# One pool of eight PSUM banks, and both query tiles of a group in one stretch, in a fused sketch-attention and mixture-of-experts attention kernel

## The chip, the cores and the metric

The kernel runs on one core of one Trainium2 chip. The metric is the device time of one execution in microseconds (us). Engines go by their names in the profile: PE (TensorE matmuls), PEld (TensorE weight loads), DVE (VectorE), ACT (ScalarE), POOL (GpSimd), SP (SyncE, which issues the DMAs).

## The reference

Two attention layers follow each other, in float32, for 4 batches of 1088 positions.

```python
# 1. polysketch attention: q, k, v (4, 4 heads, 1088, 32), S1, S2 (8, 32)
phi(x) = outer(S1 @ x, S2 @ x)            # 64 features per position
kv = sum_s phi(k) v^T;  z = sum_s phi(k)
x = (phi(q) @ kv) / (phi(q) @ z + 1e-6)   # heads side by side: (4, 1088, 128)

# 2. four attention experts of head size 64, the two best of them for each position
w = softmax over the two largest of x @ w_gate (sum + 1e-9)
for e in range(4):
    s = causal(x wq[e] @ (x wk[e])^T / 8)
    a = exp(s - max(s));  a /= sum(a) + 1e-9
    out += w_e * (a @ (x wv[e]) @ wo[e])  # w_e is 0 where e was not chosen
```

All four experts are computed for all positions, and the gate multiplies. The output is (4, 1088, 128).

## The kernel before

**Tiles.** The 1088 queries of a batch are nine tiles `i` of 128 (the last, tile 8, has 64). Tile `i` sees `n = 128 * i + 128` keys. The four experts are two groups `g` of two; the two experts `e` of a group lie in the two halves of the partitions of `qk`. Tiles 0 to 7 go in pairs `p` (tiles `2p` and `2p + 1`). For a pair and a group the kernel does the following.

- `scores`: PE multiplies queries by keys in pieces of up to 512 keys into a PSUM tile `sc` (L412). `soften` makes DVE add the causal mask, negate and keep the running minimum `mx` in one pass that also copies the tile to `a` in SBUF (L395), and ACT take the exponential with the sum `z` (L398).
- `turns_of`: PE transposes `a` by blocks of 128 into PSUM tiles `tp` (L477); `evacuate` copies each to `aT`, every third on DVE (L70), the others on ACT (L72).
- `values`: PE multiplies `aT` by the values `vt` into `av[:, 0:256]` (L552).
- `gates`: DVE makes `r = 1 / (z + 1e-9)` (L497, L498), POOL multiplies it by the gate weights into `rb` (two buffers, L501), PE transposes `rb` into `av[:, 256:]` (L507) and ACT copies that to `rs` (L509). DVE multiplies `av` by `rs` into `yT` (L557).
- `output`: PE multiplies `yT` of both groups by `wo` into `po` (L619), a copy to `ob`, and SP issues the write (L624).

Tile 8 has steps of its own: `scores_last` (L449, minimum L464, exponential L466) with both groups in one tile of 128 partitions, and `last_unit`. Pair 0 has `scores_first` (L429).

**PSUM.** The pool `ps_sc` has two tiles of two banks, for scores alone. The pool `ps_tp` has four tiles of one bank, for `tp`, `av`, `po` and everything that the first layer and the projections put there. Tiles of a pool take turns: a new tile waits until the users of the tile that had its place are done.

**Order.** PE's order is written out by hand (`manual_schedule`); a scheduler orders the other engines by the dependences. `prepare(b)` makes the next batch's first layer and projections into pieces with costs (`fill`): `kps`, `qps` (L251, sketches), `kv`, `tq`, `num`, `tx`, `qk` and `vg` (L338). `spend` puts pieces between the transposes, in proportion to the costs in `STEPS`. `units(b)` gives a batch's steps in order, by kind:

- "Q": pair 0, both groups. "P": pair 1, one group. "G": pair 2 or 3, one group. "L": tile 8.
- In the last batch pairs come in the order 1, 3, 2, 0, and "A" and "B" are the two tiles of a "G" as steps of their own.

In a "G" step PE does the scores of the first tile, then `values` of the step before, the scores of the second tile, the outputs of the step before and the transposes of the first tile with pieces between them, then the transposes of the second tile. "Q", "P", "L", "A" and "B" leave their transposes, or half of them, to the next step (`turns`, `turning`).

Of the kernel before, what the change touches and what calls it, by code (L numbers as in the profile page):

```python
# [19 lines left out]
def kernel(  # L20
# [20 lines left out]
    nc = tc.nc  # L41
# [14 lines left out]
    ps_sc = ctx.enter_context(tc.tile_pool(name="ps_sc", bufs=2, space=bass.MemoryType.PSUM))  # L56
    ps_tp = ctx.enter_context(tc.tile_pool(name="ps_tp", bufs=4, space=bass.MemoryType.PSUM))
# [9 lines left out]
    def evacuate(out_, in_):  # L67
        turn[0] += 1
        if turn[0] % 3 == 0:
            nc.vector.tensor_copy(out_, in_)  # L70
        else:
            nc.scalar.copy(out_, in_)  # L72

# [132 lines left out]
    def prepare(b):  # L206
# [7 lines left out]

        def bank(name):
            return ps_tp.tile([128, 512], F32, tag="tp", name=name)
# [176 lines left out]
    def soften(a, src, msk, mx, z, most=3e38):  # L393

        nc.vector.tensor_tensor_reduce(out=a, in0=src, in1=msk, scale=-1.0, scalar=most,  # L395
                                       op0=ALU.add, op1=ALU.min, accum_out=mx)
        if z is not None:
            nc.scalar.activation(out=a, in_=a, func=ACTF.Exp, bias=mx, scale=-1.0, accum_out=z)  # L398

    def scores(b, i, g, qk, z):  # L400

        n = 128 * i + 128
        if n <= 512:
            t = ps_sc.tile([128, 2, 512], F32, tag="sc", name=f"sc{b}_{i}_{g}")
            sc = [t[:, e, :] for e in range(2)]
        else:
            sc = [ps_sc.tile([128, 1024], F32, tag="sc", name=f"sc{b}_{i}_{g}_{e}") for e in range(2)]
        for c0 in range(0, n, 512):
            c1 = min(c0 + 512, n)
            for e in range(2):  # L410
                rows = slice(64 * e, 64 * e + 64)
                nc.tensor.matmul(sc[e][:, c0:c1], qk[rows, g, 128 * i : 128 * i + 128], qk[rows, NG + g, c0:c1],  # L412
                                 start=True, stop=True)
        mx = p4.tile([128, 2], F32, tag="mx", name=f"mx{b}_{i}_{g}")
        width, tag, bufs = (512, "as", 8) if n <= 512 else (S, "a", 4)
        ats = [p4.tile([128, width], F32, tag=tag, name=f"a{b}_{i}_{g}_{e}", bufs=bufs) for e in range(2)]
        for e in range(2):
            soften(ats[e][:, 0:n], sc[e][:, 0:n], mask[:, 1024 - n :], mx[:, e : e + 1], z[:, e : e + 1])
        return ats

    def scores_first(b, qk, zs):

        made = [[[], []] for _ in range(NG)]
        for g in range(NG):
            t = ps_sc.tile([128, 2, 512], F32, tag="sc", name=f"sc{b}_0_{g}")
            for i in range(2):
                for e in range(2):
                    rows = slice(64 * e, 64 * e + 64)
                    nc.tensor.matmul(t[:, e, 128 * i : 256 * i + 128], qk[rows, g, 128 * i : 128 * i + 128],  # L429
                                     qk[rows, NG + g, 0 : 128 * i + 128], start=True, stop=True)  # L430
            mx = p4.tile([128, 2, 2], F32, tag="mx0", name=f"mx{b}_0_{g}")
            a = [p4.tile([128, 512], F32, tag="as", name=f"a{b}_0_{g}_{e}", bufs=8) for e in range(2)]
            for i in range(2):
                for e in range(2):
                    n, dst = 128 * i + 128, a[e][:, 128 * i : 256 * i + 128]
                    soften(dst, t[:, e, 128 * i : 256 * i + 128], mask[:, 1024 - n :], mx[:, i, e : e + 1],
                           zs[g][:, i, e : e + 1])
                    made[g][i].append(dst)
        return made

    def scores_last(b, qk, z):

        sc = [ps_sc.tile([128, 1024], F32, tag="sc", name=f"sc{b}_8_{e}") for e in range(2)]
        ext = [ps_tp.tile([128, 512], F32, tag="tp", name=f"ext{b}_{e}")[:, 0:64] for e in range(2)]

        def some(dst, e, c0, c1):
            rows = slice(64 * e, 64 * e + 64)
            for g in range(NG):
                nc.tensor.matmul(dst[64 * g : 64 * g + 64], qk[rows, g, 1024:], qk[rows, NG + g, c0:c1],  # L449
                                 start=True, stop=True)  # L450

        for e in range(2):
            some(ext[e], e, 1024, S)
        for c in range(0, 1024, 512):
            for e in range(2):
                some(sc[e][:, c : c + 512], e, c, c + 512)
        mx = p4.tile([128, 4], F32, tag="mx8", name=f"mx{b}_8")
        ats = [p4.tile([128, S], F32, tag="a", name=f"a{b}_8_{e}") for e in range(2)]
        for e in range(2):
            soften(ats[e][:, 1024:], ext[e], mask_last, mx[:, 2 + e : 3 + e], None)  # L460
        for e in range(2):

            most = mx[:, e : e + 1]
            nc.vector.tensor_tensor_reduce(out=ats[e][:, 0:1024], in0=sc[e], in1=mask[:, 0:1].to_broadcast([128, 1024]), scale=-1.0,  # L464
                                           scalar=mx[:, 2 + e : 3 + e], op0=ALU.add, op1=ALU.min, accum_out=most)
            nc.scalar.activation(out=ats[e], in_=ats[e], func=ACTF.Exp, bias=most, scale=-1.0, accum_out=z[:, e : e + 1])  # L466
        return ats

    def turns_of(name, i, ats, aT, q0):

        def some(e0, e1, j0, j1):
            tp = ps_tp.tile([128, 512], F32, tag="tp", name=f"tp{name}_{e0}_{j0}")
# [54 lines left out]
    STEPS = (4.2, 2.0, 2.4, 2.4, 2.2, 3.2, 3.2, 4.1)  # L527

    def units(b, qk, vt, gw, gw8):

# [4 lines left out]
        for p in range((NJ - 1) // 2) if b < B - 1 else (1, 3, 2, 0):  # L535
            yT = p2.tile([128, NG, 256], F32, tag="yT", name=f"yT{b}_{p}")
            nk = 2 * (2 * p + 2)
            four = []
            for g in range(NG):
                if p or not g:  # L540
                    aT_all = p2.tile([128, 16 * 256], F32, tag="aT", name=f"aT{b}_{p}_{g}")
                aT = aT_all[:, 0 if p else g * nk * 256 :][:, 0 : nk * 256].rearrange("p (e j s) -> p e j s", e=2, s=256)
# [3 lines left out]
                def values(p=p, g=g, aT=aT, yT=yT, name=name):  # L546
                    av = ps_tp.tile([128, 512], F32, tag="tp", name=f"av{name}")
# [17 lines left out]
                def make(x, p=p, g=g, z=z):  # L565
                    return scores(b, 2 * p + x, g, qk, z[:, x])

                def turns(made, x, p=p, aT=aT, name=name):
                    return turns_of(f"{name}_{x}", 2 * p + x, made[x], aT, 128 * x)

                if p == 0:
                    four.append((z, turns, close))
                elif p == 1:
                    yield "P", make, turns, [close]
                elif b < B - 1:
                    yield "G", make, turns, [close]
                else:
                    yield "A", make, turns, []
                    yield "B", make, turns, [close]
            if four:  # L580
                yield ("Q", lambda x: scores_first(b, qk, [z for z, _, _ in four]),
                       lambda made, x: [f for g in range(NG) for i in range(2) for f in four[g][1](made[0][g], i)],
                       [close for _, _, close in four])
# [3 lines left out]
    def last_unit(b, qk, vt, gw8):  # L587
# [5 lines left out]
        def values():  # L593
            av = ps_tp.tile([128, 512], F32, tag="tp", name=f"av{b}_8")
# [16 lines left out]
        return ("L", lambda x: scores_last(b, qk, z[:, 0]), lambda made, x: turns_of(f"{b}_8", NJ - 1, made[0], aT, 0),  # L611
                [lambda: (gates(f"{b}_8", z, gw8[:, None, :], 128), values)])

    def output(b, p, yT):
        nq, n = (128, 2) if p < NJ // 2 else (64, 1)
        po = ps_tp.tile([128, 512], F32, tag="tp", name=f"po{b}_{p}")
# [10 lines left out]
    with tc.manual_schedule(engines={mybir.EngineType.PE}):  # L627

        warm = ps_tp.tile([128, 512], F32, tag="tp", name="warm")
# [14 lines left out]
        for b in range(B):  # L644
# [13 lines left out]
            else:  # L658
                fill.extend(own)
                lead = sum(c for c, _ in fill) / 2  # L660
            for n, (kind, make, turned, close) in enumerate(units(b, *now)):
                jobs, turns = turns + done, []
                if kind == "L" or kind == "Q" and b == B - 1:
                    for f in jobs:
                        f()
                    jobs = []
                    groups += turning
                    turning = []
                made = {x: make(x) for x in ((0, 1) if kind == "P" else (1,) if kind == "B" else (0,))}
                ends = do_values()  # L670
                spend(0.0, columns=True)
                if kind == "G":
                    made[1] = make(1)
                    jobs += turned(made, 0)
                done = [f for finish, to_gate in ends for f in finish(to_gate)]
                if b + 1 < B:
                    us = share * STEPS[n] + (lead if n == 0 else 0.0)
                else:
                    us = (lead, 1e9, 0.0)[min(n, 2)]
# [13 lines left out]
                for f in turns[:cut]:  # L693
                    f()
# [41 lines left out]
```

## Time and profile before

| what | us |
|---|---|
| median of 3 runs | 398.3 (398.27 to 398.81) |
| the profiled execution | 398.61 |
| its span, first to last instruction | 396.8 |
| PE busy in it | 373.2 (94%) |
| DVE busy | 234.6 (59%) |
| ACT busy | 226.5 (57%) |
| granted TensorE clock, mean | 1.000 |

The span is a little shorter than the execution around it. A row such as `L398 ACT ACTIVATE a<-a,mx 128x256 ... x128 | 98.1, 767 | 59.6 <-DVE mx` reads: line and engine, the operation, what it writes from what, the shape, how many; total busy time in us and the mean of one in ns; then the engine's idle time right before these and what ended most of it. In the list of waits the three numbers are the sum, the number and the longest. In the timeline a row has its start, its length, and in brackets the idle time ahead of it and what ended it. In the chain of waits a row has start, length and the work.

### The profile page before, as it was taken

The numbers are of one execution on the slowest core, as the hardware profiler recorded it, in microseconds if no ns is written. First come the engines' busy times: TensorE is split into PE (matmuls) and PEld (weight loads), VectorE is DVE, ScalarE is ACT, GpSimd is POOL, SyncE is SP. The second block draws the span as 40 slices with busy tenths as digits, with TensorE's granted clock in tenths as the row PEclk, the third lists the DMA queues.
The fourth block names the chain that finished last, engine by engine and source line by source line (L and its number), as shares of the span: only waits on it lengthen the run. The fifth ranks groups of instructions, "written<-read, shape, count | busy, mean of one in ns | idle before, by whom it ended". The sixth has DMA issues, their size and how long they took to land.

```text
span 396.8 us, 8017 instructions
## 1 busy us (share of the span) xinstructions
PE 373.2 (94%) x3152; PEld 265.4 (67%) x3152; DVE 234.6 (59%) x661; ACT 226.5 (57%) x550; POOL 58.7 (15%) x87
## 2 busy tenths in 40 slices
PE   8898999999999999999999999999999999999995
PEld 7764687667665776767664767766756475666673
DVE  6867866555548675366456564555655844745551
ACT  2236666555666656456475656754665565656582
POOL 3400461000001740000000541000000010000010
PEclk9999999999999999999999999999999999999999
DMA  7705022000000000000000000000000000000000
GB/s 192 200 2 170 16 98 71 2 1 15 13 2 0 15 2 5 15 0 15 1 15 0 2 13 7 13 2 0 15 13 2 1 16 6 0 15 2 15 4 26
DMA packets 11349, 9.95 MB, mean 25 GB/s; under 512 B 3632, under 2 KB 10288, under 8 KB 11312
## 3 DMA queue, kind: packets, MB, share of 16 engines
q1 hardware_dynamic: 11296, 9.44, 8.6%
q8 instruction: 24, 0.39, 0.4%
q14 instruction: 13, 0.11, 0.1%
q10 hardware_dynamic: 16, 0.00, 0.0%
HBM read 7.22 MB, written 2.23 MB: 24 GB/s over the span
## 4 chain that ended last, share of the span: by engine, by line
PE 72%; DVE 15%; ACT 9%; issue 2%; DMA 2%; SPq 0%; ACTq 0%; DVEq 0%
PE av L552 16%; PE sc L412 15%; PE tp L477 14%; DVE a L395 7%; ACT a L398 7%; PE qk L326 5%; PE vg L338 3%; PE num L300 3%; PE po L619 3%; PE av L600 3%; PE sc L449 2%; DMA qin<-in_q_dram 2%; DVE qT L223 1%; PE sc L429 1%; PE qps L251 1%
## 5 line engine op out<-in xcount | busy, mean ns | idle before, releaser
L398 ACT ACTIVATE a<-a,mx 128x256 f32<-128x256 f32 (+7 forms) x128 | 98.1, 767 | 59.6 <-DVE mx L395 59.2
L395 DVE CUSTOM_DVE_ANT_0 a<-sc,mask 128x256 f32<-128x256 f32 (+7 forms) x128 | 90.2, 754 | 64.1 <-PE sc L412 62.1
L477 PE MATMUL tp<-ident,a 128*128 128x128 f32 (+1 forms) x648 | 90.1, 276 | 10.6 <-DVE yT L557 6.8
L477 PEld LDWEIGHTS tp<-ident,a 128*128 128x128 f32 (+1 forms) x648 | 72.8, 142 | 26.0 <-DVE yT L557 10.2
L72 ACT COPY aT<-tp 128x512 f32<-128x512 f32 (+3 forms) x119 | 61.6, 544 | 17.9 <-PE tp L477 17.2
L552 PE MATMUL av<-aT,vt 128*64 128x256 f32 (+1 forms) x640 | 67.9, 362 | 0.0
L412 PE MATMUL sc<-qkT 64*128 64x512 f32 (+3 forms) x320 | 67.7, 541 | 0.0
L501 POOL TENSOR_TENSOR rb<-gw,r 128x256 f32<-128x256 f32 (+1 forms) x36 | 21.1, 589 | 297.2 <-DVE r L498 227.2
L552 PEld LDWEIGHTS av<-aT,vt 128*64 128x64 f32 x640 | 43.2, 137 | 31.0 <-issue 10.0
L70 DVE COPY aT<-tp 128x512 f32<-128x512 f32 (+3 forms) x61 | 38.6, 633 | 21.4 <-PE tp L477 21.3
L412 PEld LDWEIGHTS sc<-qkT 64*128 64x128 f32 x320 | 27.9, 186 | 23.7 <-issue 19.9
L326 PE MATMUL qk<-xT,wqk 128*128 128x512 f32 x64 | 31.1, 602 | 0.0
L509 ACT COPY rs<-av 128x256 f32<-128x256 f32 (+1 forms) x36 | 12.1, 356 | 27.7 <-PE av L507 27.6
L398 ACT ACTIVATION_READ_ACCUMULATOR a<-a,mx 128x1 f32 x128 | 23.9, 187 | 0.0
L619 PE MATMUL po<-wo,yT 128*128 128x128 f32 (+1 forms) x144 | 20.4, 281 | 1.7 <-DVE yT L557 1.5
L338 PE MATMUL vg<-wvg,xT 128*128 128x260 f32 (+1 forms) x72 | 20.2, 392 | 1.5 <-DVE vt L70 1.5
L497 DVE TENSOR_SCALAR r<-z 128x4 f32<-128x4 f32 (+1 forms) x36 | 6.3, 176 | 23.5 <-ACT a L398 16.6
L72 ACT COPY qkT<-qk 128x512 f32<-128x512 f32 x20 | 11.7, 585 | 14.4 <-PE qk L326 14.1
L619 PEld LDWEIGHTS po<-wo,yT 128*128 128x128 f32 (+1 forms) x144 | 17.3, 185 | 3.5 <-DVE yT L557 1.9
L300 PE MATMUL num<-kvz,qpT 128*128 128x66 f32 x144 | 17.9, 273 | 0.2 <-ACT qpT L72 0.2
L300 PEld LDWEIGHTS num<-kvz,qpT 128*128 128x128 f32 x144 | 17.1, 192 | 0.9 <-ACT qpT L72 0.5
L326 PEld LDWEIGHTS qk<-xT,wqk 128*128 128x128 f32 x64 | 10.7, 190 | 8.4 <-issue 4.7
(118 smaller groups left out, 392.0 us busy)
## 6 DMA issues: line engine op xcount, KB each, us to landing
kin<-in_k_dram SPq DMA_DIRECT2D x4, 544.0 KB, 4.0
qin<-in_q_dram SPq DMA_DIRECT2D x4, 544.0 KB, 5.1
vin<-in_v_dram SPq DMA_DIRECT2D x16, 128.0 KB, 5.7
out_dram<-ob SPq DMA_DIRECT2D x16, 128.0 KB, 1.8
vtl<-in_v_dram SPq DMA_DIRECT2D x8, 16.0 KB, 3.4
wqk<-in_moe_wq_dram SPq DMA_DIRECT2D x1, 128.0 KB, 5.3
wqk<-in_moe_wk_dram SPq DMA_DIRECT2D x1, 128.0 KB, 3.2
wvg<-in_moe_wv_dram SPq DMA_DIRECT2D x1, 128.0 KB, 3.1
```

The costliest lines, as they stand in the source:

```text
L70: nc.vector.tensor_copy(out_, in_)
L72: nc.scalar.copy(out_, in_)
L300: nc.tensor.matmul(num[:, 66 * (y - 2 * x0) : 66 * (y - 2 * x0) + 66], qpT[:, y], kvz[:, y % 2].rearrange("p h d -> p (h d)"), start=True, ...
L326: nc.tensor.matmul(t, wt(a), xT[:, 512 * c : 512 * c + 512], start=True, stop=True)
L338: nc.tensor.matmul(t[0:m, 0 : E * HD + E], xT[:, 128 * j : 128 * j + m], wvg, start=True, stop=True)
L395: nc.vector.tensor_tensor_reduce(out=a, in0=src, in1=msk, scale=-1.0, scalar=most, op0=ALU.add, op1=ALU.min, accum_out=mx)
L398: nc.scalar.activation(out=a, in_=a, func=ACTF.Exp, bias=mx, scale=-1.0, accum_out=z)
L412: nc.tensor.matmul(sc[e][:, c0:c1], qk[rows, g, 128 * i : 128 * i + 128], qk[rows, NG + g, c0:c1], start=True, stop=True)
L477: nc.tensor.transpose(tp[0:nk, x : x + 128], ats[e][:, 128 * j : 128 * j + nk], ident)
L501: nc.gpsimd.tensor_tensor(out=rb[:, 0 : w // 128].rearrange("p x (e d) -> p x e d", d=HD), in0=gws[:, :, :, None].to_broadcast(wide), in1= ...
L552: nc.tensor.matmul(av[HD * e : HD * e + HD, lo:256], vt[:, j, c : c + HD], aT[:, e, j, lo:256], start=(j == 0), stop=(j == 2 * p + 1))
L619: nc.tensor.matmul(po[0:nq, DM * x : DM * x + DM], yT[:, g, 128 * x : 128 * x + nq], wo_sb[:, g], start=(g == 0), stop=(g == NG - 1))
```

## The change

There is one pool `ps` of eight one-bank tiles, taken in turn in the order of allocation, for everything that lies in PSUM. The scores of a tile are cut into chunks of 512 keys, each with a bank of its own and a pass of its own on DVE, `take`; its minimum starts from that of the chunk before (`mx[:, e, 0:1]`). `soften` is then the exponential alone, after the last chunk. Tile 8's scores are three such chunks.

A step makes the scores of both tiles of its pair in one stretch, before `values`. Pair 1 is one step with both groups, as pair 0 was, so a batch has seven steps. The steps of pairs 0 and 1 are now of kind "G" too: every step but "L" does its own transposes, half of them between the pieces and half after. "L" still leaves its own to the next step. The last batch has the same steps as the others, in its own order of pairs.

```diff
-    ps_sc = ctx.enter_context(tc.tile_pool(name="ps_sc", bufs=2, space=bass.MemoryType.PSUM))
-    ps_tp = ctx.enter_context(tc.tile_pool(name="ps_tp", bufs=4, space=bass.MemoryType.PSUM))
+    ps = ctx.enter_context(tc.tile_pool(name="ps", bufs=8, space=bass.MemoryType.PSUM))
...
+    def bank(name):
+        return ps.tile([128, 512], F32, tag="bank", name=name)
...
-    def soften(a, src, msk, mx, z, most=3e38):
-        nc.vector.tensor_tensor_reduce(out=a, in0=src, in1=msk, scale=-1.0, scalar=most,
+    def take(dst, src, msk, mx, most=3e38):
+        nc.vector.tensor_tensor_reduce(out=dst, in0=src, in1=msk, scale=-1.0, scalar=most,
                                        op0=ALU.add, op1=ALU.min, accum_out=mx)
-        if z is not None:
-            nc.scalar.activation(out=a, in_=a, func=ACTF.Exp, bias=mx, scale=-1.0, accum_out=z)
+
+    def soften(a, mx, z):
+        nc.scalar.activation(out=a, in_=a, func=ACTF.Exp, bias=mx, scale=-1.0, accum_out=z)
 
     def scores(b, i, g, qk, z):
         n = 128 * i + 128
-        if n <= 512:
-            t = ps_sc.tile([128, 2, 512], F32, tag="sc", name=f"sc{b}_{i}_{g}")
-            sc = [t[:, e, :] for e in range(2)]
-        else:
-            sc = [ps_sc.tile([128, 1024], F32, tag="sc", name=f"sc{b}_{i}_{g}_{e}") for e in range(2)]
-        for c0 in range(0, n, 512):
-            c1 = min(c0 + 512, n)
+        mx = p4.tile([128, 2, 2], F32, tag="mx", name=f"mx{b}_{i}_{g}")
+        width, tag, bufs = (512, "as", 8) if n <= 512 else (S, "a", 4)
+        ats = [p4.tile([128, width], F32, tag=tag, name=f"a{b}_{i}_{g}_{e}", bufs=bufs) for e in range(2)]
+        for c in range(0, n, 512):
+            keys = slice(c, min(c + 512, n))
+            sc = [bank(f"sc{b}_{i}_{g}_{c}_{e}")[:, 0 : keys.stop - c] for e in range(2)]
             for e in range(2):
                 rows = slice(64 * e, 64 * e + 64)
-                nc.tensor.matmul(sc[e][:, c0:c1], qk[rows, g, 128 * i : 128 * i + 128], qk[rows, NG + g, c0:c1],
+                nc.tensor.matmul(sc[e], qk[rows, g, 128 * i : 128 * i + 128], qk[rows, NG + g, keys],
                                  start=True, stop=True)
...
-        for e in range(2):
-            soften(ats[e][:, 0:n], sc[e][:, 0:n], mask[:, 1024 - n :], mx[:, e : e + 1], z[:, e : e + 1])
+            for e in range(2):
+                m = mx[:, e, c // 512 : c // 512 + 1]
+                take(ats[e][:, keys], sc[e], mask[:, 1024 - n + c : 1024 - n + keys.stop], m,
+                     mx[:, e, 0:1] if c else 3e38)
+                if keys.stop == n:
+                    soften(ats[e][:, 0:n], m, z[:, e : e + 1])
...
-    STEPS = (4.2, 2.0, 2.4, 2.4, 2.2, 3.2, 3.2, 4.1)
+    STEPS = (4.2, 4.4, 2.4, 2.2, 3.2, 3.2, 4.1)
...
-                if p == 0:
-                    four.append((z, turns, close))
-                elif p == 1:
-                    yield "P", make, turns, [close]
-                elif b < B - 1:
-                    yield "G", make, turns, [close]
-                else:
-                    yield "A", make, turns, []
-                    yield "B", make, turns, [close]
...
+                def make(p=p, g=g, z=z):
+                    if p == 0:
+                        return scores_first(b, g, qk, z)
+                    return [scores(b, 2 * p + x, g, qk, z[:, x]) for x in range(2)]
...
+                makes.append(make)
+                turned.append(turns)
+                closes.append(close)
+                if p > 1 or g == NG - 1:
+                    yield "G", makes, turned, closes
+                    makes, turned, closes = [], [], []
...
-                made = {x: make(x) for x in ((0, 1) if kind == "P" else (1,) if kind == "B" else (0,))}
+            for n, (kind, makes, turned, closes) in enumerate(units(b, *now)):
+                made = [make() for make in makes]
                 ends = do_values()
                 spend(0.0, columns=True)
-                if kind == "G":
-                    made[1] = make(1)
-                    jobs += turned(made, 0)
+                jobs = turns + done
                 done = [f for finish, to_gate in ends for f in finish(to_gate)]
...
+                groups += turning
+                turns, turning = [f for t, m in zip(turned, made) for f in t(m)], []
+                late = turns[len(turns) // 2 :] if kind == "G" else []
+                if kind == "G":
+                    jobs += turns[: len(turns) // 2]
+                    turns = []
```

Chunk by chunk the parts of `scores_first` (now once per group) and `scores_last` change in the same way; `close`, `values` and `output` are as before but for the pool.

## The prediction

> **What bounds the kernel now.** I read first the page's busy line and the shares of the chain that ended last, then PE's waits, then all waits, then instruction forms by width, then the timeline of one step. PE is busy for 94% of the span, at a granted clock of 1.000, and the output DMAs and SP's queue do not appear in the chain: time is PE's instructions plus PE's holes.
>
> ```profile
> PE 373.2 (94%) x3152; PEld 265.4 (67%) x3152; DVE 234.6 (59%) x661; ACT 226.5 (57%) x550; POOL 58.7 (15%) x87
> ...
> PE 72%; DVE 15%; ACT 9%; issue 2%; DMA 2%; SPq 0%; ACTq 0%; DVEq 0%
> ```
> ```profile
> PE tp L477 <- DVE yT L557: 6.8, 11, 0.8
> PE kps L251 <- ACT aT L72: 1.6, 3, 0.8
> PE po L619 <- DVE yT L557: 1.5, 2, 0.8
> PE vg L338 <- DVE vt L70: 1.5, 2, 0.7
> ```
> The largest wait of PE is that of a transpose tile `tp` for `yT`, which it does not read: it needs the PSUM bank. The timeline of tile 7's step shows it.
> ```profile
> 103.58 0.37 ACT L509 COPY rs<-av 128x256 f32<-128x256 f32 x1 [2.33 <-PE av L507]
> ...
> 104.54 1.15 ACT L398 ACTIVATE a<-a,mx 128x1024 f32<-128x1024 f32 x1 [0.58 <-DVE mx L395]
> 105.50 0.08 DVE L395 DVE_READ_ACCUMULATOR2_ANT mx<- 128x1 f32 x1
> 105.50 0.42 DVE L557 TENSOR_TENSOR yT<-av,rs 128x256 f32<-128x256 f32 x1
> ...
> 105.98 0.66 PE L477 MATMUL tp<-ident,a 128*128 128x128 f32 x4 [0.77 <-DVE yT L557]
> ```
> `rs` was ready at 103.95, but `yT` stood on DVE behind two minimum passes of 1.22 us and ran at 105.50; the bank of `av`, four allocations back, came free only then. Adding the spaces between PE's records over the whole timeline gives 20.2 us: 4.3 before 22 us (the first loads), 8.4 in the twelve "G" steps of batches 0 to 2 (3.2, 2.65, 2.6), 3.8 in their "Q" and "P" steps, 3.75 in the last batch.
>
> **The change, part by part.**
>
> *One pool of eight banks (removes stalls).* Before, two pools: scores had two tiles of two banks, all else shared four. Now a bank waits for its user eight allocations earlier. I followed the changed kernel's order of instructions on each engine, with durations from the rows, through the four G steps of a batch. The first transposes reach banks that takes (the minimum passes) freed at least 1 us earlier; `av`, with its late `yT`, is needed again only a step later. So the 8.4 us go. What is late next is the exps in front of `rs` on ACT, below. I count 8.4 and give 1.2 back (15%) for places where my order is finer than my durations.
>
> *Both tiles in one stretch (removes borders).* PE's blocks of scores, in the chain and in the timeline:
> ```profile
> 96.17 1.70 PE sc L412 x8
> 97.87 3.39 PE av L552 x32
> 101.26 1.97 PE sc L412 x8
> ```
> ```profile
> 96.09 0.30 PEld L412 LDWEIGHTS sc<-qkT 64*128 64x128 f32 x4 [0.17 <-issue]
> ...
> 96.63 0.19 PEld L412 LDWEIGHTS sc<-qkT 64*128 64x128 f32 x2 [0.23 <-issue]
> 97.06 0.19 PEld L412 LDWEIGHTS sc<-qkT 64*128 64x128 f32 x2 [0.23 <-issue]
> ```
> Weight loads of 512-key matmuls follow each other every 0.43 us (96.63 to 97.06); the same view gives 0.32 for 384 keys. A 1024-key block is 4 x 0.435 = 1.74 but took 1.97; an 896-key block 2 x 0.435 + 2 x 0.32 = 1.51 but took 1.70. A border costs about 0.2 us. Five blocks per batch disappear into a neighbour (four G steps, one P): 20 x 0.2 = 4.0 us gained. Matmuls stay the same in number and shape, 3152. As a bound, the gain may be 0 if the border is an artefact of the modelled ends, and 6 if the block's other side saves too.
>
> *More minimum passes (adds DVE work).* Tiles of 640 to 1024 keys now take two chunks instead of one: 4 tiles x 2 experts x 2 groups x 4 batches = 64 more; the last 64 queries take three instead of two, 8 more. Each has its READ_ACCUMULATOR: 144 instructions.
> ```profile
> L395 DVE CUSTOM_DVE_ANT_0 a<-sc,mask 128x1024 f32<-128x1024 f32 x16 | 19.0, 1222 | 19.7 <-PE sc L412 19.7
> ...
> L395 DVE DVE_READ_ACCUMULATOR2_ANT mx<- 128x1 f32 x136 | 11.3, 83 | 0.0
> L395 DVE CUSTOM_DVE_ANT_0 a<-sc,mask 128x512 f32<-128x512 f32 x16 | 10.4, 688 | 0.0
> L464 DVE CUSTOM_DVE_ANT_0 a<-sc,mask,mx 128x1024 f32<-128x1024 f32 x8 | 10.0, 1282 | 5.0 <-PE sc L449 5.0
> ```
> Two of 688 less one of 1222 is 154 ns, and a read is 83: 72 x 0.237 = 17 us, 234.6 to about 252. A carried minimum as scalar operand is seen in L464 alone: 1282 against 1222, so 0.06 more for each of 72 at most, 4 us. [...] I put it at nothing, because DVE then runs 64% and its cover is its wait for scores (62.1 us in the trace), and because it can start a 1024-key tile after its first pair of matmuls instead of after the tile. In a G step of tiles 6 and 7, eight takes are 6 x 0.61 + 2 x 0.48 = 4.6 us (pitch in a row, since reads overlap), begin 0.9 after the first score, and end near 5.5; scores (3.5) and values (3.4) keep PE until about 6.9, when the first new bank beyond `av` is asked for. The margin is about 1.4 us, smaller where DVE is behind with copies.
>
> *P and Q in their own step (moves).* All eight blocks of tiles 2 and 3 now come at once and their transposes no longer wait for the next step. The stalls there now sum to 3.8; I find about 2.8 after. Batch 0's Q: the first transpose waits 1.4 for exps of its own scores, since the takes stand behind the STREAM_TRANSPOSEs of `kT` and `qT`, in place of 1.5 at `vg`. Batch 0's P: 0.4, a bank held by an `aT` copy behind such a transpose. Batches 1 and 2: about 0.5 each, because three `rb` now meet two buffers: the third, on POOL (612 ns), waits for PE to turn the first, and PE's turning of the third waits for POOL. The 0.3 to 0.8 waits of `kps` go. Net -1.0; bounds +3 (ACT's eight exps of P are 4 x 0.79 + 4 x 0.90 = 6.8 us, were they all waited for once) and -3.
>
> *Last batch.* A and B steps become G. 3.75 becomes about 3.6: 2.1 where tile 5's takes need `a` buffers (four) that the last queries' tiles hold until their transposes, 0.5 for a third `rb`, 0.8 and some at the closing `po`. Net -0.15. The SP queue issues the same loads and writes; the last write is still that of pair 0, so the 3.35 us after PE's last record stay.
>
> *Sum.* -8.4 - 4.0 + 0 - 1.0 - 0.15 = -13.5. The profiled execution took 398.61 (span 396.8 and 1.8 around it): 385.1. The median of the runs is 0.3 below it: 384.8. With the 1.2 given back: **386.0**.
>
> **The rivals.**
>
> *Half of the stalls come back through ACT.* The changed order has all four exps of a G step ahead of `rs` (two before), eight in P. [...] For: ACT's 57%. Against: `po` is asked for after the filling pieces, and the bank of `av` is seven allocations away. If `po` and late banks cost half of what they did, 8.4/2 and the 1.0: 391.
>
> *The merge saves nothing.* If the borders are in the records only, or the order of eight still ties a `tp` to a `yT` (P's second tile does meet one), the 4.0 is missing: 390.
>
> *DVE becomes the releaser: slower.* Every scores bank now waits for a take, and every transpose for the last chunk's exp. There are 20 merged steps; the sum's 13.5 is used up when each waits 0.67 us on average. A DVE 2.1 us later than my timelines (1.4 margin and 0.67) would do it: three or four copies of 0.69 ahead of the takes. At 2.3 us, a wait of 0.9: 384.8 + 18 = 403. [...] Against: DVE's 62 us of idle time ahead of scores.
>
> **How the numbers follow.** Forecast 0.60 (381.5 to 389.5 with the bounds of merge and P); stalls through ACT 0.14; no merge gain 0.07; DVE slower 0.16; gains and losses that cancel 0.03. Faster by over 0.2% (0.8 us, about what a measurement here can tell from no change) 0.81, within it 0.03, slower 0.16. The range 381.5 to 396 holds the first three cases and leaves out most of the slower one.
>
> **What would show it.** Right: "tp <- yT" nearly gone from PE's waits; PE's spaces 10 to 12 us instead of 20.2; PE busy near 369; DVE near 252 to 256 with some 805 instructions; no G wait for `mx` or `a` of over 0.3. Wrong: PE's scores or transposes wait for takes (`a`, `mx`) or exps in most G steps; `po` waits for `yT` more than 1.5 us in all; PE busy still 373; or Q and P waits above 5 us.

## The result and the profile after

The changed kernel takes 377.34 us (median of 4 runs, 375.66 to 378.47), against 398.28: a ratio of 0.9468, 95% interval 0.9428 to 0.9508. It is 21 us faster. The forecast was 386.0 with a range of 381.5 to 396.0: right in direction, nine us short, and outside its range. The profiled execution took 376.68 us, its span 374.9 instead of 396.8. The median stands some 1.6 us high, since two of the four runs had a granted clock of 0.99 (spans of 376.1 and 376.2, against 373.9 and 374.9), and in the profiled one the last write landed 3.12 us after its issue, where that of the kernel before took 1.84.

The busy line of the page and PE's largest waits in the kernel after:

```profile
PE 360.9 (96%) x3152; PEld 266.9 (71%) x3152; DVE 242.6 (65%) x805; ACT 227.3 (61%) x550; POOL 58.6 (16%) x87
```
```profile
PE tp L470 <- ACT a L399: 1.9, 2, 1.0
PE av L500 <- POOL rb L494: 1.6, 3, 0.5
...
PE tp L470 <- ACT aT L71: 0.9, 1, 0.9
...
PE po L607 <- DVE yT L550: 0.8, 1, 0.8
```

The wait of `tp` for `yT` (6.8 us before) is gone. What is left was mostly foreseen: three waits for a third `rb`, two in the last batch around the last queries' tiles, the closing `po`. PE's idle time over the whole trace is 9.3 us instead of 20.2. But PE is also busy 12.3 us less with the same 3152 instructions, and I had forecast 4.

The step of tile 7 in batch 0, whose stall the prediction showed, in the timeline of after (start, length, work):

```profile
97.48 0.35 ACT L502 COPY rs<-av 128x256 f32<-128x256 f32 x1
97.86 0.30 PEld L337 LDWEIGHTS vg<-wvg,xT 128*128 128x128 f32 x2
97.97 0.60 PE L337 MATMUL vg<-wvg,xT 128*128 128x260 f32 x2
97.97 0.39 DVE L550 TENSOR_TENSOR yT<-av,rs 128x256 f32<-128x256 f32 x1
98.19 0.58 PEld L470 LDWEIGHTS tp<-ident,a 128*128 128x128 f32 x4
98.41 0.60 PE L470 MATMUL tp<-ident,a 128*128 128x128 f32 x4
```

`yT` now runs beside `vg`, and the transposes no longer wait for it. They start 0.44 us after the start of `vg` (98.41 less 97.97). Here is the same pair in the timeline of before; the row of the transposes stands in the prediction, at 105.98:

```profile
104.60 0.60 PE L338 MATMUL vg<-wvg,xT 128*128 128x260 f32 x2
```

There the transposes started 1.38 us after `vg`. The stall cost 1.38 - 0.44 = 0.94 us. Its row says `0.77`. PE's record of `vg` is 0.60 long, while in the kernel after the next instruction started 0.44 after its start; the idle time counts from the record's end, so 0.16 us of the wait is booked as busy.

Counting instead from the start of each PE record to the start of the next, by the tile that the first of them writes, the two traces differ by:

| tile written | before, us | after, us | change | of that, visible as idle time |
|---|---|---|---|---|
| `tp` | 83.2 | 76.2 | -7.0 | -3.4 |
| `vg` | 22.8 | 16.8 | -6.0 | -4.3 |
| `tq` | 13.4 | 8.9 | -4.5 | -3.5 |
| `kps`, `qps` | 19.6 | 17.1 | -2.5 | -1.3 |
| `po` | 19.3 | 16.9 | -2.4 | -1.6 |
| `sc`, `ext`, `av` | 165.9 | 165.1 | -0.8 | +2.5 |
| the rest | 67.8 | 67.8 | 0.0 | +0.7 |
| all | 392.1 | 368.8 | -23.2 | -11.0 |

The time after PE's last start grew by 1.3, the late last write of this one execution, which gives the span's -21.9. None of the work that this table shows as much faster (`tp`, `vg`, `tq`, `kps`, `qps`, `po`) was changed. It lost waits.

### The profile page after: what moved, and what is told of

Read it like the earlier page. It is cut to its first block, busy times and chain, and to the rows that moved or that the text cites. A ratio compares the mean times of both kernels' runs of the same rounds, so it can differ in the third digit from the quotient of the medians.

```text
span 374.9 us, 8231 instructions
## 1 busy us (share of the span) xinstructions
PE 360.9 (96%) x3152; PEld 266.9 (71%) x3152; DVE 242.6 (65%) x805; ACT 227.3 (61%) x550; POOL 58.6 (16%) x87
## 5 line engine op out<-in xcount | busy, mean ns | idle before, releaser
L399 ACT ACTIVATE a<-a,mx 128x256 f32<-128x256 f32 (+8 forms) x136 | 107.4, 791 | 64.7 <-DVE mx L394 64.7
L470 PE MATMUL tp<-ident,a 128*128 128x128 f32 (+1 forms) x648 | 86.4, 274 | 2.9 <-ACT a L399 1.9
L394 DVE CUSTOM_DVE_ANT_0 a<-sc,mask 128x512 f32<-128x512 f32 (+3 forms) x136 | 74.0, 593 | 17.6 <-PE sc L412 12.5
L470 PEld LDWEIGHTS tp<-ident,a 128*128 128x128 f32 (+1 forms) x648 | 74.0, 142 | 13.4 <-issue 4.1
L71 ACT COPY aT<-tp 128x512 f32<-128x512 f32 (+3 forms) x122 | 63.3, 547 | 21.2 <-PE tp L470 20.1
L545 PEld LDWEIGHTS av<-aT,vt 128*64 128x64 f32 x640 | 43.3, 137 | 27.5 <-DVE mx L394 7.7
L412 PE MATMUL sc<-qkT 64*128 64x512 f32 (+3 forms) x320 | 62.4, 529 | 0.0
L69 DVE COPY aT<-tp 128x512 f32<-128x512 f32 (+3 forms) x58 | 36.3, 626 | 21.3 <-PE tp L470 21.2
L394 DVE CUSTOM_DVE_ANT_0 a<-sc,mask,mx 128x512 f32<-128x512 f32 (+3 forms) x72 | 38.3, 571 | 0.0
L71 ACT COPY qkT<-qk 128x512 f32<-128x512 f32 x17 | 9.9, 585 | 14.0 <-PE qk L325 13.8
L394 DVE DVE_READ_ACCUMULATOR2_ANT mx<- 128x1 f32 x216 | 18.3, 85 | 0.0
L550 DVE TENSOR_TENSOR yT<-av,rs 128x256 f32<-128x256 f32 x32 | 12.7, 409 | 8.6 <-ACT rs L502 4.6
(113 smaller groups left out, 386.0 us busy)
```

Source lines behind the costliest of these rows:

```text
L394: nc.vector.tensor_tensor_reduce(out=dst, in0=src, in1=msk, scale=-1.0, scalar=most, op0=ALU.add, op1=ALU.min, accum_out=mx)
L412: nc.tensor.matmul(sc[e], qk[rows, g, 128 * i : 128 * i + 128], qk[rows, NG + g, keys], start=True, stop=True)
L470: nc.tensor.transpose(tp[0:nk, x : x + 128], ats[e][:, 128 * j : 128 * j + nk], ident)
L545: nc.tensor.matmul(av[HD * e : HD * e + HD, lo:256], vt[:, j, c : c + HD], aT[:, e, j, lo:256], start=(j == 0), stop=(j == 2 * p + 1))
```

## The experiments

Theories when the first four were set up. Theory 1: the gain is the freed banks, and a wait costs more than its idle time. Theory 2: the gain is the order, with merged scores whose borders cost more than 0.2 us.

As the median of the changed kernel stands high, small differences are read beside PE's stretch from its first score to its last start in each trace: 365.1 us in the kernel before, 342.2 in the changed one. In the twelve other kernels the median lies 32.2 to 33.7 us above this stretch, in the changed kernel 35.1. It is one trace of each, and spans of one kernel's runs differ by about 1 us at clocks within 0.001 of each other (373.9 and 374.9 in the changed one).

**Pool and order, crossed.** `pool_only` has the order of before (`units` and the loop), with the new pool, and with `take`, `soften` and the three kinds of scores in chunks as in the change:

```diff
-    ps_sc = ctx.enter_context(tc.tile_pool(name="ps_sc", bufs=2, space=bass.MemoryType.PSUM))
-    ps_tp = ctx.enter_context(tc.tile_pool(name="ps_tp", bufs=4, space=bass.MemoryType.PSUM))
+    ps = ctx.enter_context(tc.tile_pool(name="ps", bufs=8, space=bass.MemoryType.PSUM))
```

> The order of before with the one pool of eight banks and one take per 512-key chunk (PE's steps Q, P, G, A, B, L and their deferred transposes as before). Theory 1, the gain is the freed banks, and a wait of PE costs more than the idle time its records show: 380 to 384 us, PE's idle time from 20.2 to some 12, and PE busy down by 6 to 9 with no matmul less. Theory 2, the gain is the order (merged scores, fewer borders): 389 to 393 us, PE busy still 371 to 373. Theory 3, takes are late in the old order: slower than 398.

Measured: 378.86 us, ratio 0.9503 (0.9486 to 0.9521). A little under Theory 1's range, and nearly the whole gain, without one merged block.

```profile
PE 366.4 (97%) x3152; PEld 267.6 (71%) x3152; DVE 241.1 (64%) x805; ACT 221.2 (59%) x550; POOL 58.5 (16%) x87
```

PE's idle time fell to 6.6 us, and its busy time by 6.8 us. PE's instructions come in the old order, but for tile 8's last 64 keys, which now come after its other keys. So these 6.8 us were waits inside records. This is Theory 1.

`two_pools` has the new order, and the pool cut in two:

```diff
-    ps = ctx.enter_context(tc.tile_pool(name="ps", bufs=8, space=bass.MemoryType.PSUM))
+    ps = ctx.enter_context(tc.tile_pool(name="ps", bufs=4, space=bass.MemoryType.PSUM))
+    ps_sc = ctx.enter_context(tc.tile_pool(name="ps_sc", bufs=4, space=bass.MemoryType.PSUM))
...
+        pool = ps_sc if name.startswith("sc") else ps
```

> The changed kernel's order with the pool cut in two again: four one-bank tiles for scores, four for all else. Theory 1 (banks): most of the gain is lost, 390 to 397 us, and the tp waits for yT are back. Theory 2 (order): 380 to 384 us. Pair 1 asks for eight scores banks at once and has four, so either theory has PE wait for takes in that step, some 1 us per batch.

Measured: 411.11 us, ratio 1.0315 (1.0295 to 1.0336), slower than either theory had it. The sum of waits of PE and of PEld for the same event:

```profile
PE sc L414 <- DVE mx L396: 4.9, 9, 0.7
```
```profile
PEld sc L414 <- DVE mx L396: 26.1, 62, 0.9
```

PE's own row shows 9 waits of 4.9 us. The row of its weight loads shows 62 of 26.1. From start to start the scores take 105.5 us against 79.3 before (`sc` and `ext`), 26.2 more, of which only 8.1 is idle in PE's records. The timeline of one step:

```profile
71.16 0.19 PEld L414 LDWEIGHTS sc<-qkT 64*128 64x128 f32 x2 [0.24 <-issue]
71.35 0.69 DVE L396 CUSTOM_DVE_ANT_0 a<-sc,mask 128x512 f32<-128x512 f32 x1 [0.36 <-PE sc L414]
71.97 0.69 DVE L396 CUSTOM_DVE_ANT_0 a<-sc,mask 128x512 f32<-128x512 f32 x1
72.10 0.29 PEld L414 LDWEIGHTS sc<-qkT 64*128 64x128 f32 x2 [0.75 <-DVE mx L396]
72.11 2.17 PE L414 MATMUL sc<-qkT 64*128 64x512 f32 x8 [0.56 <-DVE mx L396]
...
72.58 0.35 DVE L396 CUSTOM_DVE_ANT_0 a<-sc,mask,mx 128x128 f32<-128x128 f32 x1
72.72 0.72 PEld L414 LDWEIGHTS sc<-qkT 64*128 64x128 f32 x5 [0.32 <-DVE mx L396]
```

A second tile's chunk (72.10) starts when the first tile's take is done, and the other expert's (72.72) 0.62 later, at the pitch of the takes. PE's row shows no idle time between the two. The single records behind the rows say what was lost there. In the changed kernel, with banks free, the matmuls of the two experts, which lie in two halves of the partitions, start 7 ns apart, and of 512 keys the next two follow 0.43 us later; in the kernel before, 181 of the 384 score matmuls of tiles 0 to 7 start within 20 ns of the one ahead of them. In `two_pools` 126 do. Here the other expert's chunk starts 0.62 us after the first, and PE's records count the time until then as busy. This is the slower rival of the prediction, DVE as the releaser, in a kernel where scores have four banks.

`chunks_only` fills the last corner: old order, chunks, two pools (the edit of `two_pools`, made on `pool_only`).

> The order of before with one take per 512-key chunk and one-bank tiles, but still two pools: four banks for scores, four for all else. It differs from the run with the old order and one pool in the pool alone. If the one pool is the gain: 396 to 402 us, the tp waits for yT back, PE's idle time near 20. If the earlier start of DVE on a chunk is the gain: 380 to 386 us.

Measured: 410.78 us, ratio 1.0304 (1.0275 to 1.0333), slower than either case had it.

```profile
PE tp L472 <- DVE yT L552: 3.4, 7, 0.7
PE tp L472 <- ACT aT L72: 2.5, 3, 1.1
PE tq L291 <- ACT ob L72: 2.4, 2, 1.2
PE vg L339 <- ACT ob L72: 2.1, 2, 1.2
```

The rotation of four banks is still there and now waits for every kind of copy; PE's idle time is 27.5 us. So chunks and takes without the one pool cost 12.5 us; from start to start 11.5 of it stand in `tp`. Whether the 72 more passes do that, the other order of DVE's and ACT's queues that they bring, or four single banks for scores in place of two double ones was not separated. The four corners:

| | two pools | one pool of eight |
|---|---|---|
| old order, whole tiles | 398.3 | not possible in one-bank tiles |
| old order, chunks | 410.8 | 378.9 |
| new order, chunks | 411.1 | 377.3 |

The pool is worth 32 to 34 us among chunked kernels; the order is worth about 1.5 with it by the medians, 2.9 by PE's stretch (345.2 in `pool_only`), and nothing clear without it.

**How many banks.** `banks7` is the changed kernel with `bufs=7`; `pool_only6` the old order with `bufs=6`.

> The changed kernel with seven banks instead of eight. Theory 1 (a bank's release paces PE, and a wait costs its idle time plus what the modelled ends cover): 379 to 384 us, with PE's lost time growing by two to three times what its idle time shows. Theory 2 (eight banks are more than the order needs): within 1 us of the changed kernel, and one wait only in pair 1's step, which asks for eight at once.

Measured: 377.24 us, ratio 0.9467 (0.9450 to 0.9485), no different from eight by the medians. PE's stretch is 344.0 us, 1.8 more than with eight, so a small price may be there. Theory 1 in the form I gave it there, that the number of banks paces PE, is not borne out: in the new order the eighth bank is worth some 2 us at most.

> The old order with one pool of six banks. If it is the sharing that helps (a bank goes to whoever comes next) and not the number of eight: within 3 us of that order with eight banks, 378 to 382 us. If tiles need the distance of eight: 388 to 396 us.

Measured: 387.78 us, ratio 0.9724 (0.9703 to 0.9745), 8.9 above eight banks. Between the two expectations: six shared banks are 23 us better than four and four, so sharing counts, and the distance too. In the trace `vg`, `tx` and `tp` again wait for copies of `ob`, `xT` and `aT` (2.9, 1.3 and 0.6 us).

**The parts of the order.** `split_tiles` puts the second tile's scores behind `values` again in the steps of pairs 2 and 3:

```diff
-                    return [scores(b, 2 * p + x, g, qk, z[:, x]) for x in range(2)]
+                    if p == 1:
+                        return [scores(b, 2 * p + x, g, qk, z[:, x]) for x in range(2)]
+                    return [scores(b, 2 * p, g, qk, z[:, 0]), lambda: scores(b, 2 * p + 1, g, qk, z[:, 1])]
```

The deferred call is made behind `values`, right after `spend(0.0, columns=True)`.

> The changed kernel, but in the steps of pairs 2 and 3 the second tile's scores come after values again. Theory 1: 16 borders of 0.2 us come back, 3 us: 379.5 to 381.5. Theory 2 (the merge is the main gain): 384 to 388 us.

Measured: 382.90 us, ratio 0.9606 (0.9589 to 0.9623). Between the two: 5.6 us above the changed kernel, 7.7 by PE's stretch (349.9). From start to start `sc` costs 3.0 us more, as the border price has it for 16 borders. `tp` costs 2.3 more, `num` 1.2 and `vg` 1.1; PE waits there for `a` (2.8 us in three waits, against 1.9 in two) and for `qpT` (1.0 against 0.2). That the second tile's exponentials come later is the likely reason, not a tested one.

`late_turns` leaves the transposes of pairs 0 and 1 to the next step:

```diff
-                    yield "G", makes, turned, closes
+                    yield "G" if p > 1 or b == B - 1 and p == 0 else "P", makes, turned, closes
```

> The changed kernel, but the steps of pairs 0 and 1 leave their transposes to the next step again (not the last step of the last batch). Theory 1: within 1.5 us of the changed kernel, 376 to 379, since only P and Q stalls of 0.5 each move. Theory 2: 380 to 384 us, if turning in the own step removes waits in most batches.

Measured: 379.15 us, ratio 0.9528 (0.9494 to 0.9561): some 1.8 above the changed kernel, with intervals that touch, but 3.8 by PE's stretch (346.0). So transposes in their own step may be worth more than Theory 1 had it. `values` then waits for takes (2.8 us in three waits), as its bank is that of a fresh chunk.

`split_pair1` makes pair 1 one step per group again (`if p > 0 or g == NG - 1`, and eight `STEPS`):

> The changed kernel with pair 1 as one step per group again. By the border price (0.2 us each) 4 x 0.2 = 0.8 us is lost and the three waits of 0.53 for the third rb are gone (1.6 and what the ends cover, 0.5): 375.5 to 377 us. If making eight banks at once is a gain of its own: 379 to 381 us.

Measured: 376.65 us, ratio 0.9452 (0.9435 to 0.9468), no different from the changed kernel by the medians. One of three `rb` waits went (1.1 us in two waits remain), and PE is busy 2.3 us longer. PE's stretch is 343.4, 1.2 more, hardly beyond the spread: the merge of pair 1 is worth little, if anything.

**Is DVE's cover real?** `half_takes` cuts each pass of 128 keys or more into two:

```diff
-        nc.vector.tensor_tensor_reduce(out=dst, in0=src, in1=msk, scale=-1.0, scalar=most,
-                                       op0=ALU.add, op1=ALU.min, accum_out=mx)
...
+            halves = [(0, w // 2), (w // 2, w)]
+        for x, y in halves:
+            nc.vector.tensor_tensor_reduce(out=dst[:, x:y], in0=src[:, x:y], in1=msk[:, x:y], scale=-1.0,
+                                           scalar=mx if x else most, op0=ALU.add, op1=ALU.min, accum_out=mx)
```

> The changed kernel with every take of 128 keys or more cut into two halves of its bank: 208 more minimum passes and as many reads, 208 x 0.236 = 49 us more on DVE (242.6 to some 292, or 77%), nothing else. If DVE is covered as the forecast said: 377 to 381 us. If banks are released by takes at the edge (the slower rival): 390 us or more, with PE waiting for mx in most steps.

Measured: 383.77 us, ratio 0.9638 (0.9614 to 0.9661), between the two: 6.4 above the changed kernel, 8.3 by PE's stretch (350.5).

```profile
PE 365.0 (96%) x3152; PEld 268.9 (70%) x3152; DVE 277.2 (73%) x1221; ACT 225.9 (59%) x550; POOL 58.5 (15%) x87
```

DVE is busy 34.6 us more, not 49: 0.17 for each added pass and read, not 0.236. Records of passes and reads overlap, which the 0.236 leaves out: in the changed kernel a read of 83 ns starts 75 before its pass's record ends, and so does the next pass. The kernel loses 0.18 us for each of these 34.6 by the medians, 0.24 by PE's stretch. The cover is not whole, and far from gone: PE waits for no `mx` in most steps (0.9 us in three waits in all).

**A better version.** `best1` takes two of the waits left in the changed kernel away:

```diff
-        rb = p4.tile([128, 2, 128], F32, tag="rb", name=f"rb{name}", bufs=2)
+        rb = p4.tile([128, 2, 128], F32, tag="rb", name=f"rb{name}", bufs=3)
...
-        ats = [p4.tile([128, S], F32, tag="a", name=f"a{b}_8_{e}") for e in range(2)]
+        if b == B - 1:
+            ats = [kin, qin]
+        else:
+            ats = [p4.tile([128, S], F32, tag="a", name=f"a{b}_8_{e}") for e in range(2)]
```

> The changed kernel with three rb buffers instead of two, and in the last batch the last queries' a written to kin and qin (free by then) so that tile 5 does not wait for a buffer. By idle time alone: 3 x 0.53 + 1.0 = 2.6 us gained. With what the modelled ends cover (0.16 per wait of a transpose): 3.3 us, 374 us. If the waits only move to what is late next (aT copies behind exponentials on ACT): under 1.5 us, 376 or more.

Measured: 372.08 us, ratio 0.9336 (0.9314 to 0.9358), faster than the changed kernel with intervals apart.

```profile
PE 360.9 (97%) x3152; PEld 268.0 (72%) x3152; DVE 242.2 (65%) x805; ACT 226.9 (61%) x550; POOL 58.6 (16%) x87
```

The three waits for `rb` and the two of the last batch fell from 3.5 us of idle time to 0.2. From start to start `av` and `tp`, which they stood behind, take 4.3 us less with 3.3 us less idle: 0.2 us hidden in each of five waits. The median moved by 5.3, but PE's stretch by 3.7 only (338.5), near the 3.3 that was expected; the rest is the changed kernel's high median.

`best2` is `best1` with every fourth copy of `evacuate` on DVE instead of every third:

> The kernel with three rb buffers and the last queries' a in kin and qin, and every fourth evacuation on DVE instead of every third (some 15 copies of 0.63 us move to ACT: DVE -9, ACT +8). Cutting takes in half cost 6.4 us for 35 us more on DVE, 0.18 us per us; by that rate 1.6 us gained, 370 to 371 us. If ACT is as close to the edge: 372 to 375 us.

Measured: 371.86 us, ratio 0.9327 (0.9307 to 0.9348), no different from `best1`. DVE is 14 us less busy and ACT 10 more, and neither shows: the price of 0.18 us per us of DVE is not the price of every us taken off it.

## Why the prediction was right or wrong

- **The banks** (8.4 us of G stalls): right. All are gone from the trace, and the old order with the new pool shows that the pool did it. The one pool is nearly the whole gain, 19.4 of 21 us with the chunks that it needs.
- **What a wait costs:** wrong, and this is the step that failed. The prediction added "the spaces between PE's records" and took that for the time lost. In the trace of before, from 22 us on and leaving scores, `values` and `kv` aside, 31 waits show 15.2 us of idle time but cost 20.1 from start to start (over the same pair of instructions without a wait), 0.16 each unseen. That is what the records of two transposes overlap when nothing waits: one is 0.27 us long and the next starts 0.11 after it. Where no idle time shows, the steps from start to start add some 3.4 more than in after. So the removed waits were priced at their visible part, and PE busy at 369 instead of 360.9. No run here shows a true end of a PE instruction; the overlap of the records (0.27 less 0.11) is enough to hide the 0.16. The table above gives the size: of 12.3 us less busy PE time 9.0 are waits (all but `sc`, `ext` and `av`) and 3.3 fall to the merge. A view of before had shown part of it:

```profile
PEld tp L477 <- DVE yT L557: 10.2, 12, 1.2
```

  The prediction used the PE row of the same wait, 6.8. The true loss lies between, since a weight load has some slack of its own (1.18 in its row for the stall that cost 0.94).
- **The merge of scores:** 4.0 forecast, 3.3 measured (`sc`, `ext` and `av` from start to start, without idle time).
- **P, Q and the last batch:** 2.8 and 3.6 us of idle time forecast after, 2.0 and 3.2 measured. The third `rb` (0.53 three times), the exponentials of tile 5 behind the last queries' `a` (1.00) and the closing `po` (0.76) came as written. The other 0.90 in the last batch is another wait than the one foreseen: the last queries' transposes wait for an `aT` copy that stands behind two exponentials on ACT. Batch 0's Q waits 0.9 instead of 1.4, and a wait in batch 0's P step did not come.
- **DVE's price:** right but for the reads' overlap. By their records, the passes take 15.4 us more and their reads 6.3, 21.7 in all, as the 17 and the 4 for carried minima have it; a carried minimum costs 60 ns:

```profile
L394 DVE CUSTOM_DVE_ANT_0 a<-sc,mask 128x512 f32<-128x512 f32 x88 | 57.1, 687 | 14.9 <-PE sc L412 10.5 <-PE sc L451 3.0 <-PE tp L470 1.4
...
L394 DVE CUSTOM_DVE_ANT_0 a<-sc,mask,mx 128x512 f32<-128x512 f32 x24 | 17.0, 747 | 0.0
```

  The engine's busy time rose by 8.0 only and not to 252, since the records of successive passes and reads overlap, by 75 ns at each read: counted once, their time rose from 102.1 to 110.4. To put this at nothing was not quite right either: by the 0.18 to 0.24 of `half_takes`, these 8 us may cost 1.4 to 1.9, an estimate.
- **The rivals:** ACT did not bring the stalls back, though four exponentials stand before `rs`; the one wait of that kind is the 0.90 in the last batch. The DVE rival is what `two_pools` shows (62 waits of PE's weight loads for `mx`, 26.1 us). With one pool it did not bind, and `half_takes` lost 6.4 us with hardly a wait for `mx`.

In sum, against the span's -21.9: idle time -11.0 (forecast -8.4, the 1.2 given back included), the merge -3.3 (-4.0), the covered part of waits -9.0 (0), the end +1.3 (0). The covered part of waits, a term that the prediction did not have, makes up nearly the whole miss of 9.5.

## What to carry to other kernels

PE's idle time was a floor here for what its waits cost (15.2 us shown, 20.1 lost), because its records overlap when nothing waits (0.27 us long, 0.11 apart): take a wait from start to start, against the same pair of instructions where nothing waits, and look at the weight loads' row for waits that PE's row does not show. PSUM pools that are cut by purpose tie each user to few banks (six shared ones were 23 us faster here than four and four); try one pool, and judge finer chunks only with it, since the same chunks were 12.5 us of loss with two pools and part of a 20 us gain with one. When the banks no longer bind, look at the small buffers (here a third `rb` and a borrowed `a`), which held another 4 to 5 us.

## What the runs showed of the hardware

- Between transposes up to 0.16 us of a wait leaves no idle time in PE's records (a record of 0.27 us, a pitch of 0.11, before and after).
- Score matmuls of the two halves of the partitions lie over each other in the trace of the changed kernel: they start 7 ns apart, with records of 0.59 us for 512 keys, and the next two follow 0.43 us later. When their banks came free one by one, as in `two_pools`, they started apart (0.62 us in the step shown), and 18.1 of the 26.2 us lost on scores are booked as busy.
- The granted clock differed between runs of one kernel. The changed kernel's four runs had spans of 373.9 and 374.9 us at a clock of 1.000 and 0.999, 376.1 and 376.2 at 0.990 and 0.989. One run of `late_turns` had 0.989 (379.8 us, the others 377.2 to 377.4), one of `half_takes` 0.992. A busier PE is not shown to be the cause: `best1`, with PE busy for 97% of the span, had 0.997 to 1.000, as had the kernel before. What makes the clock dip in one run and not in the next was not tried.
